# Byte offsets of the moving operands, a load time in the planner, and the order of the last double steps in a three-stage fp32r kernel

## The chip, the cores and the metric

The kernel runs on one core of a Trainium2 chip. The metric is the device time of one launch in microseconds, as the median of three runs. All times below that begin with a start time come from one profiled execution of the kernel before.

## The reference

Local attention plus attention on a fourfold downsampled sequence gives x of 2304 tokens by 512. Two feed-forward blocks follow; the second gives the output.

```
x = out_up + out_local                                   # 4 x 576 tokens, 8 heads of 64
h = np.maximum(np.maximum(x @ w1, x @ w2), x @ w3)       # 512 -> 768
x = (h @ w_out).astype(np.float32)                       # 768 -> 512
h = x @ w_in                                             # 512 -> 2048
g = np.maximum(0.01 * h, h)
out = (g @ w_out).astype(np.float32)                     # 2048 -> 512
```

## The kernel before, in words

Every float32 operand of a large product is held as a high part and a rest (xh and xl, hh and hl, the two halves of gs), and each product is summed of three terms on TensorE.

**Units.** The tokens go through attention and the first feed-forward block in eight units u = 0 to 7 of 288 tokens. For each unit `L1_mm` issues 18 groups of 12 matmuls with 288 columns (line 923, 216 in all): the weights wA are stationary and xh or xl moves, four slices (kk) of each. `L2_mm` issues 72 more (line 955, into ps_o), in which hh or hl moves. The function `placed` (line 297) sets where in its tile of the pool an operand begins: X_AT and H_AT give the byte offset, mod 256, for each unit. xh and xl have two buffers each, which the units take in turn; hh and hl have one. A buffer is 4736 bytes for xh and xl, so the two buffers of one operand are 128 bytes apart mod 256, and so are neighbouring slices of 1152 bytes. In unit 4 the twelve products of a group are sorted: slices 0 and 2 first, then 1 and 3.

**The second feed-forward block.** Its first GEMM (line 1150, moving xop, 384 columns, into ps_x, ps_y, ps_z) and its second (L4, line 1191) are done by a scheme of seven products in place of eight, so that operands are sums of blocks. In L4 the stationary operand is gs and the weights w2 move, 256 columns at a time. Four supers of 512 tokens take eight steps each (i = 0 to 31, 42 matmuls a step: seven banks acc0 to acc6, six each). A last super of 256 tokens takes four double steps (i = 32 to 35), each for two of the eight parts p, three matmuls for a part and bank. Before, double steps 32 to 34 take part p through all seven banks, then part p + 1; step 35 takes both parts in a bank before the next bank.

**What a step needs.** For step i, SP loads g from DRAM into gr (line 1166, three buffers: load i waits for the copy gs of step i - 3). DVE sums blocks of gr (`gr<-gr`, three operations), ACT rounds them to the high part (line 1174, ACTIVATE gs), and DVE subtracts for the rest (`gs<-gr,gs`). gs has four buffers: that of step i comes free when PE is through with step i - 4.

**End of a super.** The seven banks are emptied by a chain: ACT copies acc0 to s1 and acc3 to s5 (line 1204); DVE forms ob from s1 and acc1, ob from s1 and acc2, s1 from ob and acc4, ob from s1 and acc5, and three more. The next super's matmuls into a bank wait for the bank's reader. Then SP stores the rows (line 1231); after the third and the fourth 512-token super these are 16 small stores.

**What sets the order.** A planner (class Plan) holds each step's engine, its assumed time, its dependences, an assumed delay from its end to its use (`after`), due times and buffers held. It makes the order of every engine's queue before anything runs. Each engine then works strictly in that order, and semaphores do the waiting. A changed number in the planner changes the order, never the work.

Of the kernel before, what the change touches and what calls it, by code (L numbers as in the profile page):

```python
# [46 lines left out]


W_AT = 64
X_AT = (112, 112, 120, 104, 16, 8, 112, 108)  # L50
H_AT = (112, 112, 120, 104, 16, 8, 24, 108)
X2_AT = ((128,) * 7, (64,) * 7, (96, 64, 96, 96, 96, 96, 96))
X2_BASE = (192, 128, 64, 0, 192, 64, 0)
NSUP = NTOK // (2 * N2)
# [47 lines left out]
class Plan:  # L102
# [13 lines left out]
    def holds(self, tag, bufs, first, last):  # L116

        self.steps[first]["tags"].append((tag, list(last)))
        self.tags[tag] = (bufs, [])
# [136 lines left out]
def local_global_attention_moe_kernel(  # L256
# [30 lines left out]
    last = {}  # L287
# [9 lines left out]
    def placed(pool, n, tag, bufs, at):  # L297
        at = at % 256 // 4
        t = pool.tile([128, NCOL * n + 32], F32R, tag=tag, bufs=bufs, name=tag)
        return bass.AP(tensor=t.tensor, offset=t.offset + at, ap=[t.ap[0], [NCOL, n], [1, NCOL]])  # L300
# [137 lines left out]
    def conv_step(t):  # L438
        if t not in conv:
            conv[t] = split_steps(wr.pop(t), sup, P, 4, lambda: scratch("0" not in PS, "mm", "wl3"))  # L440
        r = next(conv[t])
        if r and t[0] == "A":
            wA[t[1:]] = r
        elif r:
            wO[t[1]] = r
        return r
# [224 lines left out]
    def pl_Q(u, h):  # L671
        ps = pl.pop((u, h, "o"))
        if u not in X:
            X[u] = (
                placed(mmp, 4, "xh", 2, X_AT[u]),
                placed(mmp, 4, "xl", 2, X_AT[u]),
            )
# [163 lines left out]
    def turn_steps(u):  # L841
        b, half = divmod(u, 2)
        whole = u == PEU and half
        groups = ((0, 3), (3, 7), (7, 9)) if half and not whole else ((0, 4), (4, 8), (8, 9))
        xh = placed(mmp, 4, "xh", 2, X_AT[u])
        xl = placed(mmp, 4, "xl", 2, X_AT[u])
        X[u] = (xh, xl)
# [49 lines left out]
    def live_bank(name):  # L897
        bank = live["mm"] = mm_bank(name)
        live["at"] = banks_taken[0]
        return bank  # L900

    def keep(n):
        w = ident.bitcast(BF16)
        for _ in range(n if "mm" in live and banks_taken[0] - live["at"] < 3 else 0):
            T.matmul(
                out=live["mm"][:, NCOL:], lhsT=w[:, :128], rhs=w[:, : 512 - NCOL],
                start=False, stop=False, skip_group_check=True,
            )

    def L1_mm(u, m, e):  # L910
        xh, xl = X[u]
        bank = live_bank("ps_h")
        ps = bank[:, :NCOL]
        terms = ((0, xh), (0, xl), (1, xh))
        order = [(wi, xx, kk) for wi, xx in terms for kk in range(KC)]
        if u == 0:
            order = [(wi, xx, kk) for kk in range(KC) for wi, xx in terms]
        elif u == 4:
            order.sort(key=lambda t: t[2] % 2)
        for n, (wi, xx, kk) in enumerate(order):  # L920
            if u == m == e == 0 and n == 6:
                keep(FIRST)
            T.matmul(  # L923
                out=ps, lhsT=wA[m, e][wi][:, kk * 128 : kk * 128 + 128], rhs=xx[:, kk],
                start=n == 0, stop=n == 3 * KC - 1
            )
        return ps

    def L1_max(u, m, e, ps):
        if m == 0 and e == 0:  # L930
            Hs[u] = (
                placed(mmp, M1, "hh", 1, H_AT[u]),
                placed(mmp, M1, "hl", 1, H_AT[u]),
            )
# [150 lines left out]
    def a_sum(t, n):  # L1085
        if n == 1:
            out, in0, in1 = t[:, 1:6:4], t[:, 1:5:3], t[:, 0:1].to_broadcast((128, 2, t.shape[2]))
        else:
            out, in0, in1 = (t[:, 4], t[:, 1], t[:, 3]) if n == 0 else (t[:, 6], t[:, 2], t[:, 5])
        V.tensor_tensor(out=out, in0=in0, in1=in1, op=ALU.subtract if n else ALU.add)  # L1090
# [65 lines left out]
    seq2 = [(c, range(p, p + SB // n)) for c, (_, n) in enumerate(sups) for p in range(0, NP, SB // n)]  # L1156
    ga, gr = {}, {}

    def A2_load(i):
        c, ps = seq2[i]  # L1160
        if i == 0:
            gr["a"] = p2["a"].tile([128, 3, 7, SB // 2], F32, tag="raw16", bufs=1, name="gr")
        gr[i] = gr["a"][:, i % 3]
        n0, n = sups[c]
        for x, p in enumerate(ps):
            nc.sync.dma_start(
                out=gr[i][:, 0:4, n // 2 * x : n // 2 * x + n // 2].rearrange("p (a t) n -> p a t n", t=2),
                in_=gd[p][:, :, n0 : n0 + n].rearrange("p a (t n) -> p a t n", t=2),
            )

    def A2_hi(i):
        where, tag = (("a", "wl"), ("e", "ga"), ("e", "gb"), ("e", "gc"))[i % 4]
        ga[i] = p2[where].tile([128, 2, 7, SB // 2], F32R, tag=tag, bufs=1, name="gs")
        A.activation(out=ga[i][:, 0], in_=gr[i], func=AF.Copy)  # L1174

    def A2_lo(i):
        V.tensor_tensor(out=ga[i][:, 1], in0=gr.pop(i), in1=ga[i][:, 0].bitcast(F32), op=ALU.subtract)
# [3 lines left out]
    def L4(i, p, j):  # L1181
        c, ps = seq2[i]
        nt = sups[c][1] // 256
        if p == 0:
            acc[c, j] = bank("yyyyxxz"[j], "acc%d" % j)
        wh, wl = w2_op("o", p, j)
        gh, gl = ga[i][:, 0, A_AT[j]], ga[i][:, 1, A_AT[j]]
        for k in range(nt):
            m = (k + p - ps[0]) * 128
            for n, (a, w) in enumerate(((gh, wh), (gh, wl), (gl, wh))):  # L1190
                T.matmul(  # L1191
                    out=acc[c, j][:, k * 256 : k * 256 + 256], lhsT=a[:, m : m + 128], rhs=w,
                    start=p == 0 and k == 0 and n == 0, stop=p == NP - 1 and n == 2, skip_group_check=True,
                )
# [44 lines left out]
    with tc.manual_schedule(engines={ET.SP, ET.PE, ET.DVE, ET.Activation, ET.Pool}):  # L1239
# [36 lines left out]
        go, holds = pn.step, pn.holds  # L1276
# [17 lines left out]
        for n in range(CONV, len(W1)):  # L1294
            f = lambda t=W1[n]: conv_step(t)
# [91 lines left out]
        for i in range(I0, NI):  # L1387
            u, hh = divmod(i, 2)
# [93 lines left out]
        for b in range(B):  # L1482
            last = [f"ta{2 * b + 1}.2"] if 2 * b + 1 >= PEU else [f"Q{2 * b + 1}.{h}" for h in range(4)]
# [51 lines left out]
        def tile_steps(kind, p, j):  # L1535
            n = 7 * p + B_AT[kind][j]
            return f"@w5{kind}{n}" if n % 2 == 0 or n == 7 * p else f"@w5{kind}{n - 1}"
# [6 lines left out]
        order = []  # L1544
# [10 lines left out]
        def stores(s, p):  # L1555
            return [f"@gs{s}.{p}.{h}{t}" for h in range(2) for t in range(2)]

        for n, (q, j) in enumerate(order):
            s, p = q
# [38 lines left out]
        for s in range(NSUP):  # L1598
# [4 lines left out]
            last = []  # L1603
# [12 lines left out]
        for p in range(NP):  # L1616
            go(f"@yb{p}", "SP", 2.6, lambda p=p: w2_back(p), [f"@wy{p}"] + ([f"@yb{p - 1}"] if p else [f"@wy{NP - 1}"]), after=5.0)
            last = []
# [8 lines left out]
        for i, (c, ps) in enumerate(seq2):  # L1627
            size = sups[c][1] / SB
            last = sups[c][0] // (2 * N2), (sum(sups[c]) - 1) // (2 * N2) + 1
            go(f"@ar{i}", "SP", 1.45, lambda i=i: A2_load(i), [y for x in range(*last) for p in ps for y in stores(x, p)] + ([f"@ar{i - 1}"] if i else [f"@xl{NSUP - 1}"]), after=2.2)  # L1630
            for n in range(3):
                go(f"@as{i}" if n == 2 else f"@as{i}.{n}", "DVE", 0.7 if n == 1 else 0.45, lambda i=i, n=n: a_sum(gr[i], n), [f"@as{i}.{n - 1}" if n else f"@ar{i}"])
            go(f"@ah{i}", "ACT", 1.75, lambda i=i: A2_hi(i), [f"@as{i}"] + (["open5"] if i % 4 else [f"@w2o{NP - 1}.1"]))
            go(f"@al{i}", "DVE", 2.06, lambda i=i: A2_lo(i), [f"@ah{i}"])
            holds("gr", 3, f"@ar{i}", [f"@al{i}"])
            if i == 0:
                holds("raw16", 1, "@ar0", ["@ar0"])
            holds(f"ga{i % 4}", 1, f"@ah{i}", [f"@H{c}.{ps[-1]}.6"])
            turns = [(p, j) for p in ps for j in range(7)]
            if i == len(seq2) - 1:  # L1640
                turns.sort(key=lambda t: t[1])
            for p, j in turns:
                name = f"@H{c}.{p}.{j}"
                go(name, "PE", 0.69 * size, lambda i=i, p=p, j=j: L4(i, p, j), prev + [f"@al{i}", tile_steps("o", p, j)], after=0.3)
                prev = [name]
                due[name] = at
                at += 0.69 * size
        for c in range(len(sups)):
            t = 0.16 + 0.54 * sups[c][1] / SB
# [29 lines left out]
        for n in pn.order(due, SHIFT, SLACK, GAP):  # L1679
            x = pn.steps[n]  # L1680
# [87 lines left out]
```

## Time and profile before

| what | value |
|---|---|
| median of 3 runs | 775.5 us (774.08 to 775.77) |
| the profiled execution | 772.97 us, of which 771.0 us span |
| PE busy | 757.0 us, 98% of the span |
| DVE, ACT, POOL busy | 587.4, 442.2, 231.9 us |
[...]
| mean length of one matmul of line 1191, start to modelled end | 277 ns |
| largest groups on PE | line 923 202.1 + 111.9 us, line 1191 173.7 us |

In the table, busy time of PE counts a matmul from its start to a modelled end, so neighbours overlap; how fast matmuls follow one another is read from the chain of waits, where one piece of n matmuls is given with its length. Work of the units ends at 415.5 us; the first GEMM of the second block lies between there and 588.3 us; L4 and the last stores fill the rest.

### The profile page before, as it was taken

The page shows a single profiled execution, that of the slowest core. Times are in us where ns is not written, and L with a number is a line of the kernel's source. Part 1 is how long each engine was busy: PE and PEld are TensorE (multiplying, and loading weights), DVE is VectorE, ACT ScalarE, POOL GpSimd, SP SyncE. Part 2 cuts the span into 40 slices and gives each one's busy share as a digit, 9 for nine tenths or more (in the row PEclk, how much of TensorE's full clock was granted, in tenths as well). Part 3 has the DMA queues.
Part 4 walks back from the last instruction along what each step waited for, and adds up shares of the span by engine and source line. Part 5 has one row for each costly group of instructions (what it writes and reads, how often), then busy time and mean ns, then how long its engine had stood idle before and what let it go on. Part 6 is the DMA issues. An engine that isn't in the chain of part 4 may idle for free.

```text
span 771.0 us, 16059 instructions
## 1 busy us (share of the span) xinstructions
PE 757.0 (98%) x5925; PEld 726.9 (94%) x5929; DVE 587.4 (76%) x1045; ACT 442.2 (57%) x1464; POOL 231.9 (30%) x221
## 2 busy tenths in 40 slices
PE   9999999999999999999999999999999999999997
PEld 6788899899899999999999999999999999999987
DVE  5898675677996894877788788767757897879682
ACT  6988549685346854223457698677678443434240
POOL 5988779787759763100000000000000000000000
PEclk9999999999999999999999999999999999999999
DMA  9972074544533112041234687977987445454422
GB/s 357 408 305 71 17 260 117 191 133 152 169 110 123 50 54 85 2 141 55 86 110 151 230 278 259 378 281 260 310 281 230 140 131 164 124 150 120 130 84 78
DMA packets 58510, 130.60 MB, mean 169 GB/s; under 512 B 5952, under 2 KB 30528, under 8 KB 58432
## 3 DMA queue, kind: packets, MB, share of 16 engines
q1 hardware_dynamic: 53680, 124.60, 48.3%
q10 hardware_dynamic: 4752, 4.98, 1.9%
q8 instruction: 46, 0.75, 0.4%
q14 instruction: 32, 0.26, 0.1%
HBM read 93.91 MB, written 35.65 MB: 168 GB/s over the span
## 4 chain that ended last, share of the span: by engine, by line
PE 78%; DVE 8%; POOL 5%; DMA 3%; issue 3%; ACT 1%; SPq 1%; DVEq 0%; ACTq 0%; POOLq 0%
PE ps_h L923 24%; PE acc L1191 16%; PE ps_y L1150 12%; PE ps_o L955 10%; PE ps_z L1150 6%; PE ps_x L1150 3%; POOL qkprod L248 3%; PE ps_sc L743 2%; DMA gr<-gd 1%; DVE gs L248 1%; DVE wl L248 1%; DVE ob L248 1%; SPq L1231 1%; DMA lk<-in_kL_dram 1%; PE ps_up L812 1%
## 5 line engine op out<-in xcount | busy, mean ns | idle before, releaser
L923 PE MATMUL ps_h<-xh,wA 128*128 128x288 f32 x1152 | 202.1, 300 | 0.2 <-ACT xh L391 0.2
L1191 PE MATMUL acc<-w,gs 128*128 128x256 f32 x1512 | 173.7, 277 | 1.7 <-DVE ob L248 1.3
L1191 PEld LDWEIGHTS acc<-w,gs 128*128 128x128 f32 x1512 | 172.2, 188 | 3.2 <-DVE ob L248 2.4
L923 PEld LDWEIGHTS ps_h<-xh,wA 128*128 128x128 f32 x1152 | 167.6, 189 | 5.5 <-issue 3.5
L923 PE MATMUL ps_h<-xl,wA 128*128 128x288 f32 x576 | 111.9, 295 | 1.0 <-POOL xl L248 0.9
L1174 ACT ACTIVATE gs<-gr 128x1792 fp32r<-128x1792 f32 x36 | 61.0, 1704 | 87.5 <-DVE gr L248 59.5
L1150 PE MATMUL ps_y<-xop,w 128*128 128x384 f32 x576 | 105.9, 336 | 0.9 <-ACT u L1121 0.9
L1150 PEld LDWEIGHTS ps_y<-xop,w 128*128 128x128 f32 x576 | 100.3, 188 | 1.3 <-ACT u L1121 1.2
L923 PEld LDWEIGHTS ps_h<-xl,wA 128*128 128x128 f32 x576 | 88.8, 189 | 1.5 <-POOL xl L248 1.4
L955 PE MATMUL ps_o<-hh,wO 128*128 128x288 f32 x384 | 79.8, 301 | 0.0
L248 DVE TENSOR_TENSOR gs<-gr,gs 128x1792 fp32r<-128x1792 f32 x36 | 72.6, 2020 | 7.1 <-ACT gs L1174 7.1
L248 POOL TENSOR_TENSOR qkprod<-lq,lk 128x1344 f32<-128x1344 f32 x24 | 73.8, 3083 | 5.3 <-issue 2.1
L484 ACT ACTIVATE qkprod<-qkprod 128x64 f32<-128x64 f32 x280 | 67.4, 252 | 6.0 <-POOL qkprod L248 4.8
L248 DVE TENSOR_TENSOR gr<-gr 128x256 f32<-128x256 f32 (+1 forms) x108 | 54.1, 511 | 21.1 <-DMA gr<-gd 19.7
L955 PEld LDWEIGHTS ps_o<-hh,wO 128*128 128x128 f32 x384 | 61.3, 189 | 2.1 <-issue 1.4
L248 DVE TENSOR_TENSOR hm<-hm,ps_h 128x288 f32<-128x288 f32 x96 | 42.9, 447 | 22.4 <-PE ps_h L923 21.8
L955 PE MATMUL ps_o<-hl,wO 128*128 128x288 f32 x192 | 56.9, 296 | 0.7 <-POOL hl L248 0.7
L484 ACT ACTIVATION_READ_ACCUMULATOR qkprod<-qkprod 128x1 f32 x280 | 55.4, 198 | 0.0
L1150 PE MATMUL ps_z<-xop,w 128*128 128x384 f32 x288 | 53.8, 336 | 0.0
L1150 PEld LDWEIGHTS ps_z<-xop,w 128*128 128x128 f32 x288 | 50.3, 188 | 0.0
L1133 ACT ACTIVATE g<-g 128x384 f32<-128x384 f32 x72 | 37.3, 520 | 22.1 <-DVE g L248 18.3
L248 DVE TENSOR_TENSOR w<-w2y,w 128x512 fp32r<-128x512 f32 (+1 forms) x64 | 38.7, 619 | 6.2 <-ACT w L1062 6.1
(143 smaller groups left out, 1192.1 us busy)
## 6 DMA issues: line engine op xcount, KB each, us to landing
gd<-g SPq DMA_DIRECT2D x96, 192.0 KB, 4.1
gr<-gd SPq DMA_DIRECT2D x32, 512.0 KB, 4.2
sqk<-in_qk_dram SPq DMA_DIRECT2D x20, 579.0 KB, 4.6
wA<-in_wa_dram SPq DMA_DIRECT2D x18, 512.0 KB, 9.6
dsrawv<-in_vP_dram SPq DMA_DIRECT2D x16, 512.0 KB, 3.6
wl<-in_w_in_dram SPq DMA_DIRECT2D x16, 512.0 KB, 3.3
wl<-in_w_out_dram SPq DMA_DIRECT2D x16, 512.0 KB, 4.9
wd<-w2y SPq DMA_DIRECT2D x8, 896.0 KB, 5.9
```

Of the source, the lines that this page charges most:

```text
L248: self.last = f(*args, **kwargs)
L484: A.activation(out=pr[:, r, j], in_=pr[:, r, j], func=AF.Copy, accum_out=sc[:, r, j : j + 1])
L743: T.matmul(out=pst[hh][:QC, c * SD : c * SD + SD], lhsT=t[rows, 0, qs] if b else raw[rows, qs, f], rhs=t[rows, 1, :], start=f == 0, stop=f ...
L812: T.matmul(out=ps[64 * hh : 64 * hh + 64, :SD], lhsT=dst[b, h, "v"][:, kc, hh], rhs=dst[b, h, "aT", kc][:, 2 * hh : 2 * hh + 2].rearrange( ...
L923: T.matmul(out=ps, lhsT=wA[m, e][wi][:, kk * 128 : kk * 128 + 128], rhs=xx[:, kk], start=n == 0, stop=n == 3 * KC - 1)
L955: T.matmul(out=ps, lhsT=wO[m][wi][:, os_], rhs=xx[:, m], start=m0 == n == 0, stop=m1 == M1 and n == len(terms) - 1)
L1133: A.activation(out=g, in_=g if src is None else blk.pop((q, src)), func=AF.Prelu, alpha=0.01)
L1150: T.matmul(out=ps, lhsT=w[:, kk * 128 : kk * 128 + 128], rhs=xx, start=j in (0, 1, 3) and n == 0, stop=n == 5, skip_group_check=True,)
L1174: A.activation(out=ga[i][:, 0], in_=gr[i], func=AF.Copy)
L1191: T.matmul(out=acc[c, j][:, k * 256 : k * 256 + 256], lhsT=a[:, m : m + 128], rhs=w, start=p == 0 and k == 0 and n == 0, stop=p == NP - 1 ...
L1231: queue.dma_start(out=bass.AP(tensor=out.tensor, offset=out.offset + row * DM, ap=[[step, (y - x) * G], [1, DM]]), in_=ob[x * G : y * G],)
```

## The change

Three edits. First, X_AT and H_AT: xh and xl of units 2 to 6, and hh and hl of units 0 to 6, begin at byte 108 mod 256 (unit 7 is there already, and xh and xl of units 0 and 1 stay at 112). With it the sorting of unit 4's products goes. Second, the planner takes 3.5 us instead of 2.2 us from the issue of a load of g to its use, for steps after 3. Third, double steps 32 to 34 are taken bank by bank, as step 35 was.

```diff
-X_AT = (112, 112, 120, 104, 16, 8, 112, 108)
-H_AT = (112, 112, 120, 104, 16, 8, 24, 108)
+X_AT = (112, 112, 108, 108, 108, 108, 108, 108)
+H_AT = (108,) * 8
...
             order = [(wi, xx, kk) for kk in range(KC) for wi, xx in terms]
-        elif u == 4:
-            order.sort(key=lambda t: t[2] % 2)
...
-            go(f"@ar{i}", "SP", 1.45, lambda i=i: A2_load(i), [y for x in range(*last) for p in ps for y in stores(x, p)] + ([f"@ar{i - 1}"] if i else [f"@xl{NSUP - 1}"]), after=2.2)
+            go(f"@ar{i}", "SP", 1.45, lambda i=i: A2_load(i), [y for x in range(*last) for p in ps for y in stores(x, p)] + ([f"@ar{i - 1}"] if i else [f"@xl{NSUP - 1}"]), after=3.5 if i > 3 else 2.2)
...
             turns = [(p, j) for p in ps for j in range(7)]
-            if i == len(seq2) - 1:
+            if len(ps) > 1:
                 turns.sort(key=lambda t: t[1])
```

The order changes on PE only in unit 4's groups and in the last super, on POOL not at all, and on DVE, ACT and SP from the last part of the kernel on. Three places follow; lines of the changed kernel are two lower from line 918 on.

DVE at the end of the first 512-token super, where its banks are emptied; gs_8195 is the copy for step 10 of before, gs_8177 that for step 9 of after. Before:

```order
L248 TENSOR_TENSOR gr_7233<-gr_7233 128x256
L248 TENSOR_TENSOR gs_8195<-gr_7233,gs_8195 128x1792
L248 TENSOR_TENSOR ob_8236<-s1_8213,acc1_7819 128x2x256
L248 TENSOR_TENSOR gr_7233<-gr_7233 128x256
L248 TENSOR_TENSOR ob_8236<-s1_8213,acc2_7827 128x2x256
L248 TENSOR_TENSOR gr_7233<-gr_7233 128x2x256
L248 TENSOR_TENSOR s1_8213<-ob_8236,acc4_7846 128x512
```

and now:

```order
L248 TENSOR_TENSOR gr_7233<-gr_7233 128x2x256
L248 TENSOR_TENSOR gs_8177<-gr_7233,gs_8177 128x1792
L248 TENSOR_TENSOR ob_8222<-s1_8199,acc1_7819 128x2x256
L248 TENSOR_TENSOR gr_7233<-gr_7233 128x256
L248 TENSOR_TENSOR ob_8222<-s1_8199,acc2_7827 128x2x256
L248 TENSOR_TENSOR gr_7233<-gr_7233 128x256
L248 TENSOR_TENSOR s1_8199<-ob_8222,acc4_7846 128x512
```

The copy for step 10 stood ahead of the chain that empties the banks; now it stands behind the chain's end. ACT's own half of that copy moves too, from ahead of its copy of acc0 to behind its copy of acc3, and SP issues the first super's stores one load earlier.

DVE behind the third 512-token super's chain (its last operation is the one that reads acc6); the sums `gr<-gr` of size 128x256, 128x2x256 and 128x256 belong to one step each. Before:

```order
L248 TENSOR_TENSOR ob<-ob,acc_8716 128x2x256
L248 TENSOR_TENSOR gs<-gr,gs 128x1792
L248 TENSOR_TENSOR gr<-gr 128x256
L248 TENSOR_TENSOR gs<-gr,gs 128x1792
L248 TENSOR_TENSOR gr<-gr 128x2x256
L248 TENSOR_TENSOR gr<-gr 128x256 x2
L248 TENSOR_TENSOR gs<-gr,gs 128x1792
```

Now, inside the chain:

```order
L248 TENSOR_TENSOR ob<-s_9040,acc_8671 128x2x256
L248 TENSOR_TENSOR ob<-s_9040,acc_8679 128x2x256
L248 TENSOR_TENSOR gr<-gr 128x256
L248 TENSOR_TENSOR gs<-gr,gs 128x1792
L248 TENSOR_TENSOR s_9040<-ob,acc_8695 128x512
L248 TENSOR_TENSOR gr<-gr 128x2x256
L248 TENSOR_TENSOR ob<-s_9040,acc_8703 128x2x256
```

and behind it:

```order
L248 TENSOR_TENSOR ob<-ob,acc_8713 128x2x256
L248 TENSOR_TENSOR gr<-gr 128x256 x2
L248 TENSOR_TENSOR gr<-gr 128x2x256
L248 TENSOR_TENSOR gr<-gr 128x256 x2
L248 TENSOR_TENSOR gr<-gr 128x2x256
L248 TENSOR_TENSOR gs<-gr,gs 128x1792
L248 TENSOR_TENSOR gr<-gr 128x256
L248 TENSOR_TENSOR gs<-gr,gs 128x1792 x2
L248 TENSOR_TENSOR gr<-gr 128x256
```

The copy for step 26 has moved into the chain, between the second and the third of its operations. Behind the chain the copies for steps 27, 28 and 29 now stand ahead of the first sum of step 30; before, that sum stood ahead of the copy for step 29.

PE at the first double step of the last super (acc0 to acc6 are the banks; a row is one part in one bank). Before:

```order
L1191 MATMUL acc0_9514<-w2_7356,gs_9369 128x256 x3
L1191 MATMUL acc1_9520<-w2_7379,gs_9369 128x256 x3
L1191 MATMUL acc2_9525<-w2_7392,gs_9369 128x256 x3
L1191 MATMUL acc3_9529<-w2_7367,gs_9369 128x256 x3
L1191 MATMUL acc4_9535<-w2_7367,gs_9369 128x256 x3
```

and now:

```order
L1189 MATMUL acc0_9514<-w2_7356,gs_9367 128x256 x3
L1189 MATMUL acc0_9514<-w2_7392,gs_9367 128x256 x3
L1189 MATMUL acc1_9524<-w2_7379,gs_9367 128x256 x3
L1189 MATMUL acc1_9524<-w2_7410,gs_9367 128x256 x3
L1189 MATMUL acc2_9533<-w2_7392,gs_9367 128x256 x3
```

PE now goes to a new bank after six matmuls instead of three.

## Rows read from the trace of the kernel before

**Rows 1.** Busy time by stretch: us, then PE, PEld, DVE, ACT, POOL, clock, DMA.
```profile
147.00:415.50 268.50, 266.97 (x2121) 258.95 (x2121) 210.85 (x382) 136.54 (x679) 114.91 (x105) 1.00 0.31 100
415.50:438.00 22.50, 21.57 (x125) 21.25 (x124) 16.83 (x29) 16.01 (x35) 0.00 (x0) 1.00 0.70 235
252.00:283.00 31.00, 31.00 (x247) 30.39 (x245) 28.00 (x51) 22.75 (x154) 21.12 (x21) 1.00 0.15 46
```

**Rows 2.** Chain of waits (start, length, count), L1 of units 2 to 7 in turn.
```profile
183.97 3.27 PE ps_h L923 x24
...
230.98 4.85 PE ps_h L923 x36
...
258.78 6.32 PE ps_h L923 x48
...
318.46 6.40 PE ps_h L923 x48
...
348.76 19.20 PE ps_h L923 x144
...
377.59 28.43 PE ps_h L923 x216
```

**Rows 3.** The same chain, L2 of units 2, 3, 5, 6 and 7 in turn.
```profile
197.05 4.88 PE ps_o L955 x36
...
245.53 4.84 PE ps_o L955 x36
...
332.63 5.65 PE ps_o L955 x42
...
367.96 9.63 PE ps_o L955 x72
...
406.02 9.50 PE ps_o L955 x72
```

**Rows 4.** Timeline where the first super ends: DVE, ACT, then PE, each by start.
```profile
628.35 2.02 DVE L248 TENSOR_TENSOR gs<-gr,gs 128x1792 fp32r<-128x1792 f32 x1
630.28 0.68 DVE L248 TENSOR_TENSOR ob<-s,acc 128x512 f32<-128x512 f32 x1
...
635.75 2.02 DVE L248 TENSOR_TENSOR gs<-gr,gs 128x1792 fp32r<-128x1792 f32 x1
...
626.75 0.58 ACT L1204 ACTIVATE s<-acc 128x512 f32<-128x512 f32 x1
...
627.80 5.11 PE L1191 MATMUL acc<-w,gs 128*128 128x256 f32 x39
633.15 7.10 PE L1191 MATMUL acc<-w,gs 128*128 128x256 f32 x58 [0.23 <-DVE s L248]
```

**Rows 5.** Timeline of PE where the third super ends.
```profile
703.77 12.40 PE L1191 MATMUL acc<-w,gs 128*128 128x256 f32 x108
```

**Rows 6.** Timeline where the fourth super ends: DVE, ACT, PE.
```profile
744.33 2.02 DVE L248 TENSOR_TENSOR gs<-gr,gs 128x1792 fp32r<-128x1792 f32 x1
746.26 1.28 DVE L248 TENSOR_TENSOR ob<-s,acc 128x512 f32<-128x512 f32 x2
...
740.52 1.71 ACT L1174 ACTIVATE gs<-gr 128x1792 fp32r<-128x1792 f32 x1 [2.00 <-PE acc L1191]
...
743.78 2.09 PE L1191 MATMUL acc<-w,gs 128*128 128x256 f32 x17
746.99 1.22 PE L1191 MATMUL acc<-w,gs 128*128 128x256 f32 x6 [1.12 <-DVE ob L248]
748.38 0.62 PE L1191 MATMUL acc<-w,gs 128*128 128x256 f32 x3 [0.17 <-DVE s L248]
749.17 7.09 PE L1191 MATMUL acc<-w,gs 128*128 128x256 f32 x60 [0.17 <-DVE ob L248]
```

**Rows 7.** Timeline behind the third super: stores on SP's queue, and DVE's wait.
```profile
711.10 7.38 SPq L1231 DMA_DIRECT2D out_dram<-ob  x16
...
722.91 0.42 DVE L248 TENSOR_TENSOR gr<-gr 128x256 f32<-128x256 f32 x1 [5.97 <-DMA gr<-gd]
```

## The prediction

> **What bounds the kernel now.** I read the busy time by stretch first, then the chain of waits, then the timelines at the places the order changes. From 147 us, where the units become bound by PE, to 415.5 us PE is busy in 266.97 of 268.50 us, and in the next 22.50 us in 21.57 [rows 1]. So PE sets the end nearly everywhere, and the change can act in two ways: matmuls that follow one another faster, and fewer waits of PE. The chain shows that the first is open. A piece of n matmuls, divided by n, gives the pace. Unit 7's L1 is one unbroken piece of 216 at 131.6 ns, unit 4's runs at 131.7, but units 2, 3, 5 and 6 at 136.3, 134.7, 133.3 and 133.3 [rows 2]. L2 shows the same: unit 7 at 131.9, units 2, 3, 5, 6 at 135.6, 134.4, 134.5 and 133.8 [rows 3]. The clock is 1.00 throughout [rows 1], and the matmuls are of one shape, so something of the operand or of its surroundings makes 1.7 to 4.7 ns. The second is seen at the ends of supers in L4: at the third PE goes on without a break, 108 products in 12.40 us, which is 113.3 ns each once the last one's run-out of 0.16 us (its 277 ns less one distance) is taken off [rows 5]. At the first and the fourth it waits [rows 4, 6].
>
> **Offsets of x.** L1 has 216 matmuls a unit. If all units come to unit 7's pace, unit 2 saves 216 x 4.6 ns = 1.00 us, unit 3 0.67, units 5 and 6 0.37 each, unit 4 nothing [rows 2]: 2.41 us. Is the offset the reason? For it: unit 7 is the only one at 108, and it is the fastest in both GEMMs. Against it: by unit 7 POOL has no work left, so its neighbours on the chip are quieter. But unit 4 runs at 131.7 ns amid the fullest stretch, with DVE busy in 28.00 and POOL in 21.12 of 31.00 us [rows 1, 2], so busy neighbours don't make the pace; the operand's address, or the order of slices, does.
>
> Unit 4 loses its sorted order and its offset 16 at once; since unit 7 has 131.6 ns in the plain order, I cost this at nothing. From above it is bounded by unit 2's pace, 216 x 4.6 ns = 1.0 us more. Below nothing there is no room, as no unit is faster than unit 7.
>
> [...]
>
> **Offsets of h.** L2 has 72 matmuls a unit: 72 x 3.7 ns = 0.27 us for unit 2, then 0.18, 0.19 and 0.13 for units 3, 5 and 6 [rows 3], with unit 4 set to nothing for want of a clean piece: 0.77 us. Units 0 and 1 lie ahead of 147 us, where other engines set the pace; nothing is counted for them.
>
> **What of it arrives.** The sum is 3.2 us. Of this 2.1 us (1.00 + 0.67 + 0.27 + 0.18) is won in units 2 and 3, ahead of a stretch in which DVE is itself busy in 28.00 of 31.00 us [rows 1] with softmax work whose start is set by loads and POOL. If PE arrives there sooner, it meets DVE sooner. I keep half, 1.05 us; the bounds are nothing and all. The 1.1 us of units 5 and 6 come behind it, where DVE waits for PE, and I keep them. Into stretch 415.5 to 438 the ACT copies of L2's banks go along with PE, so I let the gain pass: PE lacks only 0.9 us there [rows 1]. Net: 2.1 us, between 1.1 and 3.2.
>
> **End of the first super.** DVE's copy gs for step 10 runs from 628.35 to 630.37, and the first ob only then, at 630.28, although ACT's s is ready at 626.75 + 0.58 = 627.33 [rows 4]. PE pays: from 627.80 to 633.15 there are 5.35 us for 39 products, which at 113.3 ns need 4.42, so 0.93 us are lost, and 0.2 more behind it [rows 4, 5]. After, the copy stands behind the chain. The first ob can then start at about 627.4, nearly 3 us earlier, and the whole wait goes: 1.1 us. What is late instead is that copy. It takes about the place of the next one before, ending at 635.75 + 2.02 = 637.8 at the latest [rows 4]; PE, two steps of 42 x 113.3 ns = 4.76 us behind 631, needs it at about 640.5. So 2.7 us of cover are left, and I cost it at nothing. The stores, which SP now issues one load earlier, have nobody waiting behind them but that step's load, and its copy is the one just costed.
>
> **End of the second and third super.** No wait of this kind was there at the third [rows 5]. There the copy for step 26 moves into the chain, between the second ob and s. It takes 2.02 us; before, sums of other steps and the previous copy stood in the same stretch. I get the third chain operation ready at about the time of before, so nothing; the upper bound is the copy's own 2.02 us.
>
> **End of the fourth super.** From 743.78 to 749.17 there are 5.39 us for 17 + 6 + 3 = 26 products, which need 2.95: 2.44 us are lost [rows 6]. The reason is DVE's copy from 744.33 to 746.35, ahead of the first ob at 746.26 [rows 6]. Why is it so late? ACT's half was ready at 740.52 + 1.71 = 742.23, and DVE came to it 2.1 us later. DVE had lost time before: it stood 5.97 us for the load of step 30, which SP could issue only behind 16 stores of 7.38 us [rows 7], with the finished copy of step 29 queued behind that first sum. After, copies 27 to 29 stand ahead of it, so gr buffers come free some 5 us sooner, and so do the loads of steps 32 to 35 on SP. ACT's half for step 34 still waits for PE to free the gs buffer ("<-PE acc" [rows 6]), so DVE's half can run from 742.2 to 744.2 instead, 2.1 us earlier. Bank by bank helps by itself: bank 1 is needed six products after bank 0, 0.68 us, instead of 0.34, and each DVE operation takes 0.64 [rows 6], so PE no longer overtakes the chain. With DVE at its old times only the first wait is left, about 1.0 of 2.44 us. I take a saving of 2.2 us, between 1.4 and 2.4.
>
> **Sum.** 2.1 + 1.1 + 2.2 = 5.4 us off the profiled execution, 772.97 us, 1.97 of it outside the span. The tail behind PE's last product is as before, as step 35 was bank by bank already. That execution is 2.5 us below the median of 775.5, so I take the difference off the median: 770.1 us.
>
> **Rivals.**
> First, the pace is not the offset's, or only in part. Then L1 and L2 keep their rows, and the ends of supers alone give 3.3 us: 772.2. Unit 4's good pace at another offset, with sorted slices, speaks for it; unit 4's DVE load, and L2 showing the same ranking, speak against.
> [...]
> [...]
> Second, the planner's new order does not shed the waits: the copy in the third chain is late and a new wait of up to 2.0 us appears there, and DVE is late at the fourth end as before, so that 1.0 us stays. Ends of supers then bring 1.1 + 1.4 - 2.0 = 0.5 us, and with the offsets it is 772.9. If the offsets also bring nothing, the change does not do what it says: 775.0.
> Third, slower: copies gs that now stand behind the chains come too late for PE. The cover at step 10 is 2.7 us. If the load behind it is held as the load of step 30 was, 5.97 us [rows 7], PE stands 5.97 - 2.7 = 3.3 us. It decides as soon as a load lands over 2.7 us late. At all three 512-token ends that is 9.9 us; against 5.4 us won this gives 775.5 + 4.5 = 780.0. Against it: one load more or less ahead of the stores is all that SP's order changes.
>
> **How the numbers follow.** Chances: forecast, with the offsets' gain anywhere from 1.1 to 3.2, 0.56; pace unchanged, 0.18; new waits at the ends, offsets good, 0.11; both fail, 0.09; slower, 0.06. The predicted time is the forecast's. Its own bounds: 3.2 + 1.1 + 2.4 = 6.7 gives 768.8, and 1.1 + 1.1 + 1.4 - 2.0 = 1.6 gives 773.9. The first two rivals at their centres lie inside. With the runs' own spread the range is 768.3 to 774.0. A measurement of this kernel tells about 0.2% from no change, 1.55 us: faster means below 773.95. The forecast, and the first two rivals in all but their upper tail, lie below: 0.81; same 0.13; slower 0.06.
>
> **What would show it.** In the trace after: L1 pieces of units 2, 3, 5, 6 at 131.6 to 132 ns and L2 at 131.9; the end of unit 7 about 2 us earlier; at the first super's end DVE's ob straight behind ACT's s and PE without a wait; at the fourth end a copy that is over before the last step of the super ends, and at most one wait of PE. I am wrong if units 2 and 3 keep 134 ns or more at 108, if unit 4 rises towards 136, if PE's wait moves to the third end, or if PE waits for a gs copy.

## The result, and the profile after

The changed kernel takes 768.94 us in the median, against 775.63 us for the kernel before in the same comparison: ratio 0.9911, 95% interval 0.9887 to 0.9935. One of the four executions of the changed kernel took 1490.14 us; it stands in this median, and the ratio leaves it out. In a second comparison it took 767.6 against 774.18 us, ratio 0.9921, interval 0.9897 to 0.9945. That is 6 to 7 us less; 770.1 was predicted, from 768.3 to 774.0. Its profiled execution took 768.03 us with a span of 766.2 us, 4.8 us less than the span before. Of these, 1.0 us lie ahead of L4, whose first product starts at 590.4 us now and started at 591.4 before (the 588.3 us given for the end of the first GEMM were too early), and 3.8 in L4. That is less than 6 to 7 us because the profiled execution of before was 2.7 us below its median and that of the changed kernel 0.9.

The busy time by stretch, after (columns as in [rows 1]; the last row is the stretch of L4):

```profile
147.00:415.70 268.70, 266.46 (x2121) 257.60 (x2122) 210.51 (x383) 136.63 (x679) 117.30 (x105) 0.99 0.31 100
415.70:438.00 22.30, 22.30 (x130) 22.17 (x130) 17.82 (x30) 16.16 (x35) 0.00 (x0) 1.00 0.73 245
590.30:766.20 175.90, 171.61 (x1514) 171.41 (x1512) 137.53 (x174) 66.92 (x52) 0.00 (x0) 1.00 0.44 127
```

The first row holds the surprise. Faster products should have made this stretch 2 us shorter, yet unit 7 ends at 415.7 us, as before (415.5). PE is not busier, and the clock is 0.99 where it was 1.00.

The chain of waits, after: first a short piece of unit 3's L1, then L1 of units 4, 5, 6, 7, then L2 of units 5, 6, 7, then L4.

```profile
218.17 3.21 PE ps_h L921 x24
...
253.23 6.32 PE ps_h L921 x48
...
319.28 6.33 PE ps_h L921 x48
...
349.28 18.96 PE ps_h L921 x144
...
377.74 28.44 PE ps_h L921 x216
...
333.25 5.55 PE ps_o L953 x42
...
368.25 9.50 PE ps_o L953 x72
...
406.18 9.49 PE ps_o L953 x72
...
590.52 170.05 PE acc L1189 x1500
```

Against [rows 2, 3] units 5 and 6 went from 133.3 ns to 131.9 and 131.7, their L2 from 134.5 and 133.8 to 132.1 and 131.9. Units 2 and 3 have no long piece on this chain any more. Taken from start to start (distances under 160 ns alone), their L1 products stood 135.1 and 134.6 ns apart before and 131.8 in both after. For unit 2 the durations of the single matmuls show it too (the line's list from 156 to 191 us; ns as least/median/most), before and after:

```profile
L923 PE MATMUL ps_h<-xh,wA x138: 292/298/403, 156.2 to 190.9; 128*128 128x288 f32 x138
```
```profile
L921 PE MATMUL ps_h<-xh,wA x140: 291/293/399, 156.0 to 190.6; 128*128 128x288 f32 x140
```

Of PE's waits in the units two of over 0.2 us are new (timeline): one for DVE's dssum (a sum of the softmax) in unit 2's L2, one for POOL's last hl of unit 3.

```profile
196.44 0.38 PE L645 MATMUL ps_lt<-ident,ple 96*102 96x96 f32 x2 [0.22 <-DVE dssum L248]
...
246.85 0.40 PE L953 MATMUL ps_o<-hl,wO 128*128 128x288 f32 x1 [0.32 <-POOL hl L248]
```

And L4 is one piece. The timeline of PE has it as a single row of 1512 products in 171.56 us, 113.4 ns from start to start, with no wait at any super's end; [rows 4, 6] showed breaks there:

```profile
590.36 171.56 PE L1189 MATMUL acc<-w,gs 128*128 128x256 f32 x1512
```

What DVE did at the fourth end after the change (timeline, answering to [rows 6]): the copy of step 34 ends at 741.96 and the two obs at 743.15, while PE comes to the next super at 742.7 (590.36 plus 1344 products of 113.36 ns) and to its second bank 0.68 us later.

```profile
739.94 2.02 DVE L248 TENSOR_TENSOR gs<-gr,gs 128x1792 fp32r<-128x1792 f32 x1 [0.88 <-ACT gs L1172]
741.88 1.27 DVE L248 TENSOR_TENSOR ob<-s,acc 128x512 f32<-128x512 f32 x2
```

### The profile page after: what moved, and what is told of

Same layout as the page of the kernel before. It is cut to its first block, busy times and chain, and to the rows that moved or that the text cites. A ratio compares the mean times of both kernels' runs of the same rounds, so it can differ in the third digit from the quotient of the medians.

```text
span 766.2 us, 16061 instructions
## 1 busy us (share of the span) xinstructions
PE 753.7 (98%) x5929; PEld 724.1 (95%) x5929; DVE 586.9 (77%) x1045; ACT 442.2 (58%) x1464; POOL 234.6 (31%) x221
## 4 chain that ended last, share of the span: by engine, by line
PE 79%; POOL 8%; DVE 6%; DMA 3%; issue 2%; ACT 2%; DVEq 0%; ACTq 0%; SPq 0%; POOLq 0%
PE acc L1189 22%; PE ps_h L921 19%; PE ps_y L1148 13%; PE ps_o L953 9%; PE ps_z L1148 7%; POOL qkprod L248 4%; PE ps_x L1148 3%; PE ps_sc L743 2%; DMA sqk<-in_qk_dram 1%; ACT qkprod L484 1%; POOL hl L248 1%; DMA lk<-in_kL_dram 1%; DVE wl L248 1%; POOL ple L248 1%; PE ps_ls L593 1%
## 5 line engine op out<-in xcount | busy, mean ns | idle before, releaser
L921 PE MATMUL ps_h<-xh,wA 128*128 128x288 f32 x1152 | 198.3, 299 | 0.2 <-ACT xh L391 0.2
L1189 PE MATMUL acc<-w,gs 128*128 128x256 f32 x1512 | 171.6, 276 | 0.0
L921 PE MATMUL ps_h<-xl,wA 128*128 128x288 f32 x576 | 108.8, 295 | 1.1 <-POOL xl L248 1.0
```

Of the source, the lines that this page charges most:

```text
L921: T.matmul(out=ps, lhsT=wA[m, e][wi][:, kk * 128 : kk * 128 + 128], rhs=xx[:, kk], start=n == 0, stop=n == 3 * KC - 1)
L1189: T.matmul(out=acc[c, j][:, k * 256 : k * 256 + 256], lhsT=a[:, m : m + 128], rhs=w, start=p == 0 and k == 0 and n == 0, stop=p == NP - 1 ...
```

## The experiments

"Before" is the kernel before, run with each group on the same chip. Where the time is told as a ratio, the interval is that of 95%.

**Offsets alone.**

```diff
-X_AT = (112, 112, 120, 104, 16, 8, 112, 108)
-H_AT = (112, 112, 120, 104, 16, 8, 24, 108)
+X_AT = (112, 112, 108, 108, 108, 108, 108, 108)
+H_AT = (108,) * 8
...
-        elif u == 4:
-            order.sort(key=lambda t: t[2] % 2)
```

> The kernel before with the offsets of x and h alone at 108 (and unit 4's sorting gone, as these go together). Theory: the offset sets the pace, so L1 and L2 of units 2, 3, 5, 6 follow at 131.5 to 132.3 ns, 3.2 us in all; but the trace of the changed kernel has unit 7's L2 beginning at 406.02 instead of 405.86, so most of it is lost between 190 and 253 us (a lower granted clock behind PE's wait at 206, and waits for POOL's hl), and only the wait at 437 us that goes is left: 0.5 to 2 us faster than before. Rival 1, the offset does nothing to the pace: 134 to 136 ns in units 2 and 3, no difference. Rival 2, the whole 3.2 us arrive when the clock holds: 3 us faster.

Measured 773.21 against 773.56 us, ratio 1.0001 (0.9987 to 1.0015): no difference, at most 1.1 us either way. The pace is that of the changed kernel in every unit; L1 of units 6 and 7 on its chain of waits:

```profile
349.48 18.96 PE ps_h L921 x144
...
377.94 28.44 PE ps_h L921 x216
```

So the first rival, an offset without effect on the pace, falls, but so does my estimate of what arrives.

**The last stage alone, and its two edits one by one.**

```diff
# e2: both; e3: the first; e4: the second
-... after=2.2)
+... after=3.5 if i > 3 else 2.2)
...
-            if i == len(seq2) - 1:
+            if len(ps) > 1:
                 turns.sort(key=lambda t: t[1])
```

> The kernel before with the last stage's two edits alone (load time in the planner, double steps bank by bank). Theory: PE's waits at the ends of the first and fourth super are gone, as in the changed kernel, and L4 runs in about 171.6 us without a break instead of 175.1: 3.5 us faster, pace of the units as before. Rival: the freed 1.3 us at 437 us also comes from this part: 4.8 us faster. Second rival: without the offsets the loads fall otherwise and a wait of about 1 us comes back: 2.5 us.

> The kernel before with the planner's load time alone. Theory: this edit does nearly all of the last stage's gain: 1.1 us at the first end, and at the fourth the copy of step 34 ends at about 744.2 instead of 746.35, so that even part by part PE waits at most 0.3 us: 3.2 to 3.5 us faster. Rival: bank by bank is what spares the fourth end: then about 1.4 us of PE's wait stay there and it is 2.1 us faster.

> The kernel before with double steps 32 to 34 bank by bank alone. Theory: the first end keeps its 1.1 us; at the fourth the late copy stays and of 2.44 us the first wait of about 1.0 is left: 1.4 us faster. Rival: the order of the planner moves with it and the copy is early too: 2.4 us. Other rival: nothing is won, as DVE's chain and not the distance of the banks sets the wait.

Both: 768.75 us, ratio 0.994 (0.992 to 0.9959), 4.6 us less. The planner's load time alone: 769.96, ratio 0.996 (0.9946 to 0.9974), 3.1 us. Bank by bank alone: 771.03, ratio 0.9968 (0.9949 to 0.9986), 2.5 us. By the traces L4 (from its first product's start to its last one's) took 175.1 us before, 171.8 with the planner's number, 173.1 bank by bank, 171.3 with both. PE at the fourth super's end, with the planner's number alone:

```profile
739.75 5.54 PE L1191 MATMUL acc<-w,gs 128*128 128x256 f32 x47
745.47 10.70 PE L1191 MATMUL acc<-w,gs 128*128 128x256 f32 x92 [0.17 <-DVE ob L248]
```

and bank by bank alone, at the first and the fourth end:

```profile
632.32 7.91 PE L1191 MATMUL acc<-w,gs 128*128 128x256 f32 x65 [0.23 <-DVE s L248]
...
746.05 10.17 PE L1191 MATMUL acc<-w,gs 128*128 128x256 f32 x86 [0.31 <-DVE ob L248]
```

The planner's number takes away the first end's waits and nearly all of the fourth's; one short wait is left there, since PE still runs through the banks faster (three products, 0.34 us, to a bank) than DVE empties them (0.64 to 0.69 us an operation). Bank by bank leaves the first end's waits (1.0 us) and cuts the fourth's three to one. The two overlap at the fourth end, so their gains don't add up.

**The changed kernel again.**

> The changed kernel again, on the chip and in the hour of the three that follow, so that they can be set beside it. By the parts measured alone (offsets no difference, last stage 4.6 us) it is 4.6 to 5.5 us faster than before; if the offsets add what units 5 to 7 show in the trace (1.0 us), nearer 5.5; if the first measurement's 6.7 us were all real, 6.7.

767.6 us, ratio 0.9921: 6.1 us less than before. The two parts alone add up to 4.6 (3.2 to 6.2 for the last stage, and nothing, give or take 1.1, for the offsets), so what the whole has beyond its parts lies within the intervals, and whether the offsets do better in its company stays open.

**Offsets dealt out anew**, all products in plain order.

```diff
-X_AT = (112, 112, 108, 108, 108, 108, 108, 108)
-H_AT = (108,) * 8
+X_AT = (112, 112, 108, 104, 120, 16, 108, 120)
+H_AT = (108, 108, 108, 104, 120, 16, 108, 120)
```

> The changed kernel with the offsets dealt out anew: x and h of unit 2 at 108, of unit 3 at 104, of unit 4 at 120, of unit 5 at 16, of unit 6 at 108, of unit 7 at 120, all with the products in plain order. Theory, the offset sets the pace: units 4 and 7 go to about 135 ns in L1 and L2 (unit 2's pace at 120 before), unit 3 to 134.6 (its own before), units 2 and 6 stay at 131.7, unit 5 at 16 shows whether unit 4 owed its 131.6 to the offset (132 again) or to its sorted order (134 or more). Rival, the pace belongs to the unit and its surroundings: unit 7 and unit 4 stay at 131.6 whatever the offset.

The chain of waits of this kernel: L1 of units 3, 4, 5, 6 and 7, then L2 of unit 7.

```profile
232.07 4.85 PE ps_h L921 x36
...
260.04 6.41 PE ps_h L921 x48
...
320.07 6.38 PE ps_h L921 x48
...
350.17 18.96 PE ps_h L921 x144
...
378.63 29.17 PE ps_h L921 x216
407.80 6.88 PE ps_o L953 x51
```

Unit 7 at 120 falls from 131.6 to 135.0 ns, its L2 to 134.9; unit 4 at 120 from 131.7 to 133.5; unit 3 at 104 is back at its old 134.7; unit 6 at 108 keeps 131.7. The pace follows the offset and not the unit, but for some 1.5 ns between units at the same offset (133.5 and 135.0 at 120). Unit 5 at 16 in plain order has 132.9, so by this comparison of two units unit 4 owed most of its good pace to that offset and perhaps 1 ns to the sorting. The time of this one execution, 771.0 us, is not compared.

**PE's waits at 204 to 206 us filled**, with 4 and 15 small matmuls into columns that nobody reads.

```diff
-KEEP_TO = 150.0
+KEEP_TO = 230.0
```

> The changed kernel with 19 small matmuls into unused columns, put into PE's two waits at about 204 to 206 us (4 and 15 of them, some 0.1 us each); all else in the same order. Theory: the lower granted clock from about 207 to 210 us follows from PE having stood still there; with the gap filled the clock stays 1.00, unit 3's L1 takes 33.3 us instead of 34.1 to 34.5, and what is not eaten by POOL later arrives: 0.3 to 1.3 us faster than the changed kernel. Rival: the clock falls all the same, and the fills, longer than the wait by up to 0.4 us, only delay: 0 to 0.4 us slower. Third: the clock holds but POOL's chain sets the pace to 253 us, so nothing is won.

768.69 us, ratio 0.9929 (0.9909 to 0.995): not faster than the changed kernel, by the medians 1.1 us slower, within the intervals. The clock did hold. Granted clock is the third number from the end; the stretches 204 to 208 and 208 to 212 us of the changed kernel:

```profile
204.00:208.00 4.00, 2.46 (x18) 1.65 (x16) 3.90 (x7) 1.62 (x5) 2.55 (x5) 0.83 0.59 185
208.00:212.00 4.00, 4.00 (x25) 4.00 (x24) 3.63 (x5) 1.40 (x8) 3.92 (x4) 0.74 0.43 127
```

and with the fill, in the same stretches:

```profile
204.00:208.00 4.00, 3.67 (x40) 3.12 (x38) 3.90 (x8) 2.04 (x6) 2.90 (x4) 1.00 0.44 119
208.00:212.00 4.00, 4.00 (x35) 3.81 (x32) 3.86 (x6) 1.44 (x7) 3.47 (x4) 1.00 0.45 128
```

With the fill, unit 3's L1 takes 32.9 us instead of 34.1. But unit 4's L1 begins 97.1 us behind unit 2's, against 97.0 in the changed kernel. So something else holds unit 4 back, and PE meets it in the products of unit 3's L2. The third of the expectations was right.

The fall of the clock does not come with the new offsets. In the three kernels above that keep the old ones it fell at the same place: from 208 to 212 us it was 0.57 with both edits and 0.83 bank by bank; here with the planner's load time alone:

```profile
204.00:208.00 4.00, 3.00 (x16) 2.36 (x17) 4.00 (x4) 1.28 (x4) 2.21 (x4) 0.72 0.65 205
208.00:212.00 4.00, 4.00 (x27) 4.00 (x27) 3.01 (x7) 1.84 (x9) 3.83 (x3) 0.86 0.47 145
```

In these three (both edits, load time, bank by bank) unit 4's L1 begins 97.0, 97.4 and 97.2 us behind unit 2's; in two profiles of the changed kernel it is 97.0 and 97.4, with the offsets alone 97.3. So where the clock falls, the new offsets win nothing between these two points. The 95.7 us of the kernel before belong to an execution in which the clock held. At a held clock no two of these kernels differ by the offsets alone.

**Products on POOL made thin**, first for unit 4, then for unit 6, then for unit 6 with the fill. In each a part of the attention is left out: two thirds of the columns of q x k.

```diff
# e7: i in (8, 9); e9 and e10: i in (12, 13)
-        P.tensor_tensor(out=pr, in0=in0, in1=in1, op=ALU.mult)
+        n = 1 if i in (12, 13) else RC
+        P.tensor_tensor(out=pr[:, :n], in0=in0[:, :n], in1=..., op=ALU.mult)
```

> The changed kernel with POOL's products q x k of unit 4 done on a third of their columns, their readers reading that third again and again: a part of the attention is left out. POOL's six operations of 3.08 us become about 1.1; its queue keeps its order. Theory: what ate the offsets' gain in units 2 and 3 is POOL, whose hl stands behind such products (PE's wait for hl at 246.85, and the late start of the units): with POOL thinner, these waits go, unit 3's L2 takes 10.4 us instead of 11.2, and unit 4's L1 begins 0.5 to 1.5 us earlier. Rival: POOL's waits are those of its loads and of DVE, not of its own work, and unit 4's L1 begins as before.

> The changed kernel with POOL's products q x k thinned to a third for unit 6, not unit 4: these are the ones that stand ahead of unit 3's last hl at 239.9 to 246.0 us (a part of the attention is left out). Theory: PE's wait for that hl (0.3 to 1.0 us, at 246.7) goes, as hl comes some 4 us sooner; unit 3's L2 takes 10.5 to 10.7 us instead of 11.6, unit 4's L1 begins 96.2 to 96.6 us behind unit 2's instead of 97.1 to 97.4, and 0.5 to 1 us of it arrive at the end. Rival: something else waits there at the same time (DVE, the loads of v), and unit 4's L1 still begins 97 us behind unit 2's.

> The same with the 19 small matmuls in PE's waits at 204 to 206 us, so that the clock holds too (the same part of the attention is left out). Theory: with the clock held and hl early both gains pass: unit 4's L1 begins 95.2 to 95.8 us behind unit 2's, and it is 1 to 1.5 us faster than the kernel with the thin products alone. Rival: a third chain (DVE's) takes over at 253 us and nothing more is won than with thin products alone.

For unit 4: 767.02 us, ratio 0.9908 (0.989 to 0.9926). These were the wrong products: the ones ahead of unit 3's last hl belong to unit 6. PE came to that hl earlier and waited 1.02 us for it instead of 0.32; unit 4's L1 began 97.6 us behind unit 2's. What stands in the way is seen in the changed kernel's chain of waits:

```profile
222.02 1.80 PE ps_h L921 x12
...
223.91 0.45 DVE hm L248
...
225.75 1.55 DVE pvprod L248
...
227.75 5.39 DMA dsrawv<-in_vP_dram
...
233.28 1.29 POOL dsrawv L248
...
234.64 0.73 POOL dsv L248
235.37 0.77 POOL hl L248
236.14 3.04 POOL qkprod L248
239.18 0.76 POOL hl L248
239.94 5.77 POOL qkprod L248 x2
...
246.00 0.80 POOL hl L248
...
246.85 4.75 PE ps_o L953 x34
```

A load of v, which waits for DVE, sets off POOL, and unit 3's last hl stands behind two products of 3 us. From 223.9 us on PE's pace does not matter to this chain; ahead of that the chain hangs on PE's products of unit 3's L1, through DVE's hm. With unit 6's products thin (POOL's timeline), hl is done at 242.47 and PE does not wait:

```profile
236.58 2.25 POOL L248 TENSOR_TENSOR qkprod<-lq,lk 128x448 f32<-128x448 f32 x2
241.66 0.81 POOL L248 TENSOR_TENSOR hl<-hm,hh 128x288 fp32r<-128x288 f32 x1 [2.83 <-ACT hh L391]
```

Unit 4's L1 then begins 94.7 us behind unit 2's (95.3 with the fill), and unit 7 ends at 413.2 us instead of 415.7. The clock held in both profiles (1.00 from 204 to 212 us). The comparison that leaves POOL alone is that of the two kernels with the fill, 95.3 against 97.1 us: the part of unit 6's products that is left out costs PE 1.8 us here. In time little of it is left: 767.45, ratio 0.9919 (0.9893 to 0.9945), and with the fill 766.68, ratio 0.9907 (0.9882 to 0.9931). A part goes at the next place: in the waits of the kernel with thin products, from 415 to 440 us, the wait at 435 us is back that the kernel before had at 437.

```profile
DVE x2r L248 <- DMA x2r<-x2d: 3.0, 1, 3.0
...
PE ps_y L1153 <- ACT u L1124: 0.9, 1, 0.9
```

There DVE stands for the reload of x, and ACT's u, and with it PE, behind DVE. That gives back about 1 us.

**hl of unit 3 ahead of the last product of unit 6 on POOL**, without and with the fill; all work is done.

```diff
-... + ([f"mu{i}.{c - 1}"] if c else []))
+... + ([f"mu{i}.{c - 1}"] if c else []) + (["hl3.5"] if (i, c) == (13, 2) else []))
```

> The changed kernel, all work done, with one dependence more in the planner: the last product q x k of unit 6's second half comes behind unit 3's last hl on POOL. The planner moves other steps of units 4 to 7 as well. Theory: hl comes about 3 us sooner, the wait at 246.7 goes, 0.3 to 0.9 us faster than the changed kernel. Rival: the moved steps of DVE and ACT cost more than that: 0 to 2 us slower.

> The same with the 19 small matmuls at 204 to 206 us. Theory: both arrive, 1 to 2 us faster than the changed kernel, the fastest of all that does the whole work. Rival: as for the kernel before it, the moved steps cost more.

769.33 us, ratio 0.9943 (0.9924 to 0.9962), and 769.2, ratio 0.9945 (0.9925 to 0.9966). Unit 4's L1 did begin earlier, 96.2 and 95.7 us behind unit 2's, but the steps that the planner moved cost PE a new wait for hl at 287.6 us in unit 4's L2. None of the kernels that do the whole work beat the changed one.

## Why the prediction was right or wrong, point by point

- **The pace at 108: right**, in every unit (131.7 or 131.8 ns in L1), and that the offset makes it is shown by the offsets dealt out anew. The rival by which the pace belongs to unit 7 falls. One size was off. I read unit 2's 136.3 ns from a piece of 24, and such short pieces read high: the one of unit 3 above, at 108, reads 133.8. From start to start unit 2 had 135.1, so its L1 had 0.7 us to win, not 1.0.
- **What of it arrives: wrong.** I kept half of units 2 and 3 and all of units 5 and 6, 2.1 us. Alone, the offsets gave no difference in time, give or take 1.1 us. The step that failed is the reading of [rows 1]: PE busy in 266.97 of 268.50 us says that PE never waited long, not that nothing else was as long. I named DVE as what PE would meet. In unit 2's L2 it was DVE: a wait of 0.2 us, and 11.9 us for the whole instead of 11.4. In unit 3's L2 it was POOL and a load, through the last hl. That wait is 0.3 to 1.0 us in the five profiles with all offsets new and POOL's work ahead of that hl untouched; the four with the old offsets have none there. From unit 2's first to unit 4's first product I kept half of 2.1 us; at a like clock (97.0 to 97.4 us with either offsets) nothing was won. I worked from a profile of 95.7 us in which the clock held, and in nearly all others without the fill it fell behind PE's waits at 204 to 206 us (to between 0.57 and 0.77 in the lower of the two stretches of 4 us, in eight profiles). Units 5 to 7 did pass their 1.0 us on: from unit 5's L1 to unit 7's end 120.1 us instead of 121.1. The time of the offsets alone does not show this 1.0 us, which lies at the edge of its interval.
- **The stretch from 415 to 438 us: mis-read.** I let the gain pass. It holds a wait of PE of 0.9 us, in a chain that begins with the reload of x. The kernel before had it, the changed kernel had not. It is not earliness of PE that brings it: with the offsets dealt out anew unit 7 ended at 417.5 us and PE waited, with unit 4's thin products it ended at 415.0 and PE did not. The reload took 6.7 to 7.0 us from its last issue to its use by DVE in the four profiles with the wait, and 5.6 to 6.2 in the other ten. Why is open.
- **End of the first super: right**, by the planner's number alone: 1.3 us by the products' starts, where I had 1.1.
- **End of the third super: right**, no wait came, and no copy was late for PE.
- **End of the fourth super: right in place, the parts mis-sized.** By the products' starts 2.6 us were lost there before and nothing after, where I had a saving of 2.2. Bank by bank alone left 0.7 us where I had 1.0. The copy of step 34 was over 0.6 us before the super's last product, about as forecast.
- **The sum: right by luck, as two errors cancel.** The last stage gave 3.8 us in the trace and 4.6 (3.2 to 6.2) in time, where I had 3.3; the offsets gave less than the 2.1. The whole was 6 to 7 us where I had 5.4. That is 1.5 to 2.3 us more than the parts measured alone add up to, within the intervals and not explained.

## What to carry to other kernels

An engine that is busy throughout a stretch need not be its only bound (PE was busy in 266.46 of 268.70 us of the changed kernel, and part of POOL's products still cost it 1.8 us with the fill): before counting a gain of pace, take the first operation behind the stretch that waits for another engine, and read how much later that other engine's chain would let it start. A planner's load time that is too short puts work whose load is late ahead of work that is ready, and mending one number was worth at least as much here (3.1 us, 2.0 to 4.2) as mending the order by hand (2.5 us, 1.1 to 3.9). Compare the granted clock of two profiles before you compare their times. And measure parts alone: a right total can hide a part that does nothing.

## What the runs showed of the hardware

- In L1, with 288 columns, the distance of back-to-back matmuls went with the byte at which the moving operand begins in its tile (mod 256): 131.7 ns at 108 (units 4 and 6 of the changed kernel), 132.9 at 16 and 134.7 at 104 (units 5 and 3 with the offsets dealt out anew), 133.5 to 135.1 at 120 (units 4 and 7 of that kernel, unit 2 of the kernel before).
- In the changed kernel the granted clock was 0.83 and 0.74 of full speed in two stretches of 4 us, the first of which has PE's waits of 0.55 and 0.99 us. From 207.5 to 210 us it was 0.50, and from 207.9 to 210.1 us the products stood 0.24 us apart. Unit 3's L1 took 34.1 us, and 32.9 with these waits filled by small matmuls. With the fill the clock was 1.00 there in the profiled execution of all three kernels that had it. Without the fill it was 1.00 in two of the profiled executions too (the kernel before, and unit 6's products thin), so the waits alone don't decide it; what does was not found.
